# Turning two quarters of x by DMA instead of TensorE, with GpSimd normalising the last, in an attention-and-gate kernel

## The chip, the cores and the metric

The kernel runs on one core of one Trainium2 chip. The metric is the device time of one launch in microseconds, as the median of several runs. The core has five engines with an instruction stream each: TensorE (PE), VectorE (DVE), ScalarE (ACT), GpSimd (POOL) and SyncE (SP, which here only issues transfers). The engines run at the same time and wait for each other by semaphores.

## The reference

x is 2048 rows by 512 columns in bf16. It is normalised row by row, and the result goes into two branches: attention with 32 query heads of width 16 that all share one key and one value head, and a dense network with 1792 hidden columns. The output joins them.

```python
xn = _layernorm(x, axis=-1)
q = (xn @ wq)          # 32 heads of 16
k = xn @ wk            # one head of 16
v = xn @ wv            # one head of 16
scores = jnp.einsum("bhqd,bkd->bhqk", q, k) * (Dh ** -0.5)
p = _softmax(scores, axis=-1)
o = jnp.einsum("bhqk,bkd->bhqd", p, v)
s = o.transpose(0, 2, 1, 3).reshape(B, S, H * Dh) @ wo
h = _silu(xn @ w1)     # 1792 columns
g = _silu(h @ w2)
return x + s * g
```

## The kernel before

**Data.** x lies in SBUF as 16 tiles of 128 rows (`x_sb`). A quarter is four tiles, 512 rows; there are four, numbered 0 to 3 by `c` in the code. Each quarter is normalised into `xn_sb`, turned so that the columns of x lie on the partitions (`xnT_sb`), and then projected: to keys (`mm_K`, in two halves of 256 rows), to values (`mm_V`), to queries and into the dense network.

**Scores and exponentials.** Heads are worked in groups of four; four quarters of queries times eight groups give 32 groups, and each meets 16 key tiles of 128 rows. One key tile for four heads is four blocks of 128 x 512 scores, so there are 2048 blocks. TensorE computes them (L613). Two blocks side by side in one of two buffers `psA` (a "pair" below) go to ScalarE, which takes the exponential of both in one instruction (L643). Single blocks in the banks `psD` (two halves) and `psF` go to VectorE, which makes exponentials another way: it adds and clamps in int16 so that the bits form a power of two (L681), and GpSimd adds two offsets to a finished tile of four blocks (`int64_add`, L706); three weighted copies of the values make the sum close to the exponential. TensorE multiplies the exponentials by the values into `psO` (L765, a "round" is four such multiplications side by side). ScalarE also takes 72 tanh of the dense network (L1081).

**The order.** Nothing is decided at run time. A recorder, the class `Sched` and the loop behind it, goes through the whole program when the kernel is built. It keeps a model of when each engine will be free and when each result will be ready, and with it writes one fixed list of instructions and waits for each engine. In each step the loop decides what TensorE does next: another pair for ScalarE, a block for VectorE if a bank is free, a round of `psO`, a piece of the dense network, or a job of the `front` list (turn T, keys K, values V, quarter by quarter). So how many blocks ScalarE takes and how many VectorE takes falls out of the recording. The numbers that steer the decisions come from a table `RULES` of 22 rows, and a string `PLAN` names a row for each stretch of 5 us of recorded time:

```python
    STRETCH = 5
    PLAN = (
        "AAAAJAVDBHQUALNMAMMPRULHALUHROAAMAKVIAVMMASMAAAAAFVIAAKAANJM"
...
RULES[PLAN[min(int(K.act_end / STRETCH), len(PLAN) - 1)]]
```

A transfer has a `lane`, its own semaphore; in the recorder's model it takes its issuing engine 0.05 us and lands after the `cost` that is given.

**The front.** Quarter 0 is handled by hand-written calls. For the others VectorE takes statistics of each tile (L408), aggregates them (L423), GpSimd forms the reciprocal standard deviation (`rstd_pow`, L427 and L429), VectorE normalises four tiles (`normalise`, L441), TensorE turns two tiles at a time against an identity (`transposes`, L452, eight transposes into one bank), VectorE copies them out (`evac_T`, L460), TensorE projects keys (`mm_K`, L483) and VectorE copies these to `kTa_sb` (`evac_K`, L495). Four transfers on SP then move them to other partitions of `kTb_sb` (`move_K`, L501), from which every second group reads. SP also issues the weight loads (w1 at L383, wo and w2 at L386 and L387) and, after the last normalisation, reloads four x tiles for the final addition (`load_xr`, L1087).

Of the kernel before, what the change touches and what calls it, by code (L numbers as in the profile page):

```python
# [13 lines left out]
P = 128  # L14
# [21 lines left out]
class Sched:  # L36
# [107 lines left out]
    def op(self, eng, fn, reads=(), writes=(), lane=None, cost=None):  # L144
        who = lane or eng
        if lane:
            self.lanes[lane] = eng
        n = self.done.get(who, 0)
        self.done[who] = n + 1
        deps = self.deps(eng, reads, writes)  # L150
        self.at[(who, n)] = self.model(eng, lane, cost, max([self.at[d] for d in deps.items()], default=0.0))
        clk = self.clock.setdefault(eng, {})
        waits = []
        cand = [(f, m) for f, m in deps.items() if clk.get(f, -1) < m]
        for f, m in cand:
            implied = False
            for f2, m2 in cand:
                if (f2, m2) != (f, m) and self.snap[(f2, m2)].get(f, -1) >= m:
                    implied = True
            if not implied:  # L160
                waits.append((f, m))
        for f, m in cand:
            for g, k in self.snap[(f, m)].items():
                if clk.get(g, -1) < k:
                    clk[g] = k
            if clk.get(f, -1) < m:
                clk[f] = m
        for f, m in waits:
            self.flagged.setdefault(f, set()).add(m)
        self.snap[(who, n)] = dict(clk)  # L170
        self.queues.setdefault(eng, []).append((fn, waits, who, n))
        for r in reads:
            self.readers.setdefault(r, {})[who] = n
        for w in writes:
            self.last_w[w] = (who, n)
            self.readers[w] = {}
        return who, n
# [36 lines left out]
def bass_recurrent_scan__grouped_kv_mqa__dense_activation_silu__prompt_kernel(  # L214
# [16 lines left out]
    NC = S // NQ  # L231
# [20 lines left out]
    EV = "vava"  # L252
    PVWAIT, FKEEP = 0.2, 0.75
    NPAIR, LEAD_PAIR = 1, 1
    TWIN = 0
    XHOLD, XTASK, XWAIT, XGAIN, XCOST, XOPEN, XBEH, AIM = 7, 0, 0.3, 9, 1.0, 0, 99, 0.43
    TGATE, FRESH, JOINT = 0.33, 0, 0
# [20 lines left out]
        K=(0.2, 3.0, 0.65, 10, 1.2, 2.0, 0, 12, 0.2, 3, 3, 0.0, 0.15, 0.43, 0, 0.33, 0, 0),  # L278
# [14 lines left out]
    with ExitStack() as es:  # L293
# [46 lines left out]
        K = Sched()  # L340
# [63 lines left out]
        def tiles(c):  # L404
            return range(4 * c, 4 * c + 4)
# [26 lines left out]
        def rstd_sqrt(c):  # L432
# [4 lines left out]
            K.act_end += 1.28  # L437
            op("v", lambda e: e.reciprocal(rstd_sb[:, sl], rstd_sb[:, sl]), reads=[("rstd", c)], writes=[("rstd", c)], cost=0.2)

        def normalise(t, eng):  # L440
            op(eng, lambda e: e.tensor_scalar(xn_sb[:, t % 8, :], x_sb[:, t, :], mv_sb[:, t, 0:1], rstd_sb[:, t:t + 1],  # L441
                                              op0=ALU.subtract, op1=ALU.mult),
               reads=[("x", t), ("mv", t), ("rstd", t // 4)], writes=[("xn", t % 8)], cost=0.41)

        def transposes(c, half, bank, key):
            ps = bank.bitcast(BF16)
# [28 lines left out]
                op("v", lambda e: e.tensor_copy(dst, src), reads=[key], writes=[("xnT", 0, t)])  # L475

        def xnT_keys(c):
            return [("xnT", c, t) for t in range(2 if c else 4)]

        def mm_K(c, bank, key, a=0, b=NQ):  # L480
            def f(e):
# [320 lines left out]
        def ln_ag(tk):  # L802
            c = tk["c"]
            for t in tiles(c):
                aggr(t)
            rstd_pow(c)
            tok.add(("ag", c))
            if c == NC - 1:
                first_add()
                for a in shifts:  # L810
                    shift(*a)
                shifts.clear()

        def ln_nm(tk):
            t = tk["t"]
            normalise(t, "v")
            tok.add(("nm", t))
            if t == NT - 1:
                for n in range(4):
                    load_xr(n)  # L820

        for c in range(1, NC):
            if c > 1:
                for t in tiles(c):
                    task("st", ln_st, 0.687, t=t, reads=[("x", t)], writes=[])
                task("ag", ln_ag, 0.4, c=c, reads=[], writes=[], need=[("st", t) for t in tiles(c)])
            for t in tiles(c):
                task("nm", ln_nm, 0.41, t=t, reads=[("rstd", c)], writes=[], need=[("ag", c)] + ([("T", t - 8)] if t >= 8 else []))

        def on_slot(gi):  # L830
# [85 lines left out]
        jobs = [jb for _, jb in timed]  # L916
        all_slots = sum(SIZE[jb[0]] for jb in jobs)
        jobs += [("wp", tt) for tt in range(4 * (NC - 1), 4 * NC)]
        front = [("V", 0)] + [jb for c in range(1, NC) for jb in (("T", c, 0), ("T", c, 1), ("K", c, 0), ("K", c, 1), ("V", c))]
        jst = dict(open=None, part=0, bank=None, tanh=[], slots=0)  # L920

        def progress():
# [26 lines left out]
        def front_ready(jb, t):  # L949
            k, c = jb[:2]  # L950
            if k == "T":
                ts = [4 * c + 2 * jb[2] + n for n in range(2)]
                return all(("nm", n) in tok for n in ts) and K.ready("pe", [("xn", n % 8) for n in ts]) <= t + 0.2
            if k == "K":
                return ("xnT",) + jb[1:] in tok and K.ready("pe", [("xnT",) + jb[1:]]) <= t + 0.2
            return (c == 0 or all(("xnT", c, h) in tok for h in range(2))) and K.ready("pe", xnT_keys(c) + ["wv"]) <= t + 0.05

        def emit_front(jb, b):
# [561 lines left out]
```

## Time and profile before

| What | Value |
|---|---|
| Median of 2 runs | 662.22 us (662.14 to 662.3) |
| The profiled execution's own time | 662.46 us |
| Its span in the profile | 660.6 us |
| Granted TensorE clock over the span | 1.0 |
| First and last start of a ScalarE exponential (L643) | 10.2 and 652.1 us |
| Exponentials on ScalarE, and its tanh | 662 and 72 |
| Score blocks evaluated by VectorE (L681, 512 columns each) | 724 |
| VectorE normalisations (L441) of quarters 1 to 3 | 12, in steps of about 0.35 us |
| VectorE copies of turned tiles (L460) of quarters 1 to 3 | 6, 0.67 to 0.69 us each |
| First weight load (w1, 1792 KB): issue, time to landing | 15.22 us, 8.1 us |

In the rows of groups, the columns are line, engine, operation, output and inputs with shapes, and count; then busy time and mean duration of one; then the engine's idle time ahead of them and who ended it. In a table of waits they are the waiting engine and line, the engine and line waited for, the total, the number of waits and the longest. In a timeline they are start, length and the instruction with its count. In a table of stretches they are the stretch and its length, busy time and count of each engine, the granted clock, the share of the DMA engines and GB/s. The chain of work is followed back from the last instruction, at each step to what released it.

### The profile page before, as it was taken

Reading aid. Unit: us, or ns where it says so; the run is one execution under the profiler, and the core shown is the slowest. Engines: PE = TensorE matmul, PEld = TensorE weight load, DVE = VectorE, ACT = ScalarE, POOL = GpSimd, SP = SyncE. Lnnn points to the kernel's source line nnn. Section 1 sums busy time; section 2 is a strip of 40 time slices with the busy share of each in tenths; the row PEclk is TensorE's granted clock in tenths of the full one; section 3 lists DMA queues with packets and bytes.
Section 4 is the critical chain, followed back from the end, with each engine's and each line's share of the span. In section 5 each row is a group of like instructions: output and inputs, shape, how many; then the busy total and the mean of one; then the engine's idle time right before and its main releaser. Section 6 shows DMA issues by size and latency. Waiting matters only on the chain.

```text
span 660.6 us, 18424 instructions
## 1 busy us (share of the span) xinstructions
PE 648.8 (98%) x8061; PEld 182.9 (28%) x8061; DVE 597.3 (90%) x1021; ACT 652.5 (99%) x754; POOL 382.9 (58%) x387
## 2 busy tenths in 40 slices
PE   8999999999999999999999999999999999999996
PEld 4422222222222222222222222222222222222222
DVE  7998899998899989999998989999989888898996
ACT  8999999999999999999999999999999999999997
POOL 3265666655566567566656655575656555665554
PEclk9999999999999999999999999999999999999999
DMA  5440000000000000000000000010000000000110
GB/s 167 153 147 1 2 1 2 2 1 2 2 1 2 17 18 18 17 2 2 1 2 1 2 1 2 2 33 18 18 1 3 1 2 2 1 2 2 33 34 33
DMA packets 12320, 12.48 MB, mean 19 GB/s; under 512 B 2512, under 2 KB 11728, under 8 KB 12240
## 3 DMA queue, kind: packets, MB, share of 16 engines
q1 hardware_dynamic: 11680, 10.78, 5.3%
q8 instruction: 63, 1.03, 0.7%
q10 hardware_dynamic: 560, 0.52, 0.2%
q14 instruction: 17, 0.14, 0.1%
HBM read 8.95 MB, written 2.10 MB: 17 GB/s over the span
## 4 chain that ended last, share of the span: by engine, by line
ACT 91%; PE 4%; DVE 2%; issue 1%; DMA 1%; SPq 1%; POOL 0%; POOLq 0%
ACT pa_sb L643 85%; ACT t_sb L1081 5%; PE psA L613 1%; DMA x_sb<-in_A_x_dram 1%; PE psO L765 1%; DVE ph_sb L681 1%; DVE stats_sb L408 0%; POOL ph_sb L706 0%; PE psD L452 0%; PE psF L392 0%; DMA kTb_sb<-kTa_sb 0%; SPq L501 0%; PE psD L483 0%; DVE kTa_sb L495 0%; POOLq L293 0%
## 5 line engine op out<-in xcount | busy, mean ns | idle before, releaser
L643 ACT ACTIVATE pa_sb<-psA 128x1024 bf16<-128x1024 f32 x662 | 630.5, 1217 | 0.9 <-PE psA L613 0.6
L706 POOL INT64_ADD ph_sb<-ph_sb x290 | 300.3, 1048 | 192.7 <-DVE ph_sb L681 192.6
L681 DVE TENSOR_SCALAR ph_sb<-psD 128x512 int16<-128x512 f32 (+1 forms) x520 | 349.1, 689 | 33.7 <-PE psD L613 29.8
L765 PE MATMUL psO<-ph_sb,vaug_sb 128*32 128x512 bf16 x1740 | 215.9, 383 | 0.1
L765 PE MATMUL psO<-pa_sb,vaug_sb 128*32 128x512 bf16 (+1 forms) x1332 | 200.2, 383 | 0.4 <-ACT pa_sb L643 0.4
L613 PE MATMUL psA<-qT_sb,kTa_sb 32*128 32x512 bf16 x688 | 133.4, 385 | 1.9 <-DVE kTa_sb L495 0.5
L613 PE MATMUL psD<-qT_sb,kTb_sb 32*128 32x512 bf16 x353 | 129.5, 384 | 0.0
L613 PE MATMUL psA<-qT_sb,kTb_sb 32*128 32x512 bf16 x628 | 121.7, 385 | 2.2 <-ACT pa_sb L643 1.7
L613 PE MATMUL psD<-qT_sb,kTa_sb 32*128 32x512 bf16 x309 | 111.6, 384 | 0.2
L706 POOL INT64_ADD x_sb<-x_sb x72 | 74.5, 1046 | 52.2 <-DVE x_sb L681 52.1
L681 DVE TENSOR_SCALAR x_sb<-psD 128x512 int16<-128x512 f32 (+1 forms) x132 | 90.1, 690 | 10.6 <-PE psD L613 8.9
L765 PE MATMUL psO<-x_sb,vaug_sb 128*32 128x512 bf16 x432 | 73.7, 383 | 0.0
L613 PEld LDWEIGHTS psA<-qT_sb,kTa_sb 32*128 32x128 bf16 x688 | 32.3, 91 | 141.8 <-ACT pa_sb L643 125.5
L392 PE MATMUL psF<-xnT_sb,w_sb 128*32 128x512 bf16 x896 | 71.1, 385 | 0.0
L392 PE MATMUL psF<-w_sb,u_sb 128*32 128x512 bf16 x896 | 69.2, 384 | 0.0
L613 PEld LDWEIGHTS psA<-qT_sb,kTb_sb 32*128 32x128 bf16 x628 | 29.5, 91 | 134.4 <-ACT pa_sb L643 124.4
L765 PEld LDWEIGHTS psO<-ph_sb,vaug_sb 128*32 128x32 bf16 x1740 | 52.5, 95 | 49.7 <-issue 34.1
L765 PEld LDWEIGHTS psO<-pa_sb,vaug_sb 128*32 128x32 bf16 x1332 | 48.1, 94 | 41.9 <-issue 32.1
L1081 ACT ACTIVATE t_sb<-psF 128x512 bf16<-128x512 f32 x72 | 57.4, 797 | 0.0
L1113 DVE SCALAR_TENSOR_TENSOR u_sb<-t_sb,psF 128x512 bf16<-128x512 bf16 x56 | 38.0, 679 | 4.7 <-ACT t_sb L1081 4.2
L681 DVE TENSOR_SCALAR ph_sb<-psF 128x512 int16<-128x512 f32 x52 | 35.4, 681 | 0.0
L613 PEld LDWEIGHTS psD<-qT_sb,kTb_sb 32*128 32x128 bf16 x353 | 30.9, 91 | 3.5 <-DVE ph_sb L681 2.5
(128 smaller groups left out, 341.6 us busy)
## 6 DMA issues: line engine op xcount, KB each, us to landing
w_sb<-in_B_w_dram SPq DMA_DIRECT2D x2, 1792.0 KB, 8.8
x_sb<-in_A_x_dram SPq DMA_DIRECT2D x18, 128.0 KB, 2.3
out_dram<-ob_sb SPq DMA_DIRECT2D x14, 128.0 KB, 1.7
x_sb<-in_A_x_dram SPq DMA_DIRECT2D x3, 512.0 KB, 7.1
wop_sb<-in_A_wo_dram SPq DMA_DIRECT2D x1, 512.0 KB, 4.0
wq_sb<-in_A_wq_dram SPq DMA_DIRECT2D x1, 384.0 KB, 6.6
x_sb<-in_A_x_dram ACTq DMA_DIRECT2D x2, 128.0 KB, 2.9
kTb_sb<-kTa_sb SPq DMA_DIRECT2D x16, 16.0 KB, 2.3
```

The costliest lines, as they stand in the source:

```text
L392: r = e.matmul(bank[32 * i:32 * i + 32, :], lhsT=lhsT[:, 32 * i:32 * i + 32], rhs=rhs, start=start, stop=stop, tile_position=(0, 32 * i), ...
L613: return e.matmul(ap, lhsT=kT_sb[g % 2][32 * i:32 * i + 32, kt * P:(kt + 1) * P], rhs=qT_sb[32 * i:32 * i + 32, c % 2, g // 2, :], start=T ...
L643: d = op("a", lambda e: e.activation(pa_sb[:, sl, :], psA[k][:, :], ACT.Exp, scale=ESCALE), reads=["A%d" % k], writes=[("pa", sl)], cost=2 ...
L681: d = op("v", lambda e: e.tensor_scalar(ph_ap(0, sl, 512 * pos, 512 * pos + m), src, float(PH_ONE + PH_BIAS), 0.0, op0=ALU.add, op1=ALU.ma ...
L706: d = op("gp", lambda e, j=j: e.int64_add(ph_ap(j, sl, 0, 4 * NQ).bitcast(I64), ph_ap(0, sl, 0, 4 * NQ).bitcast(I64), PH_SHIFT[j] * 0x0001 ...
L765: r = e.matmul(psO[32 * i:32 * i + 32, cs], lhsT=vaug_sb[:, p["v"], p["kt"], :], rhs=p["ap"], start=s0, stop=s1, tile_position=(0, 32 * i) ...
L1081: op("a", lambda e: e.activation(t_sb[:, n % 2, :], bank_ap(b), ACT.Tanh, scale=0.5 if jb[0] == "h" else 0.25), reads=[b], writes=[("t", n ...
L1113: op("v", lambda e: e.scalar_tensor_tensor(out=dst, in0=t_sb[:, n % 2, :], scalar=1.0, in1=src, op0=ALU.add, op1=ALU.mult), reads=tk["read ...
```

## The change

Quarters 2 and 3 (the third and the fourth; `TR`) are no longer turned by TensorE. Each normalised tile of 128 x 512 is turned by one transposing transfer on SP, straight from `xn_sb` to its place in `xnT_sb`; the T jobs of these two quarters and their copies by VectorE are gone. The recorder is told that such a transfer lands after 2.6 us. The four tiles of quarter 3 (`GNORM`) are normalised by GpSimd, right behind its reciprocal deviation, instead of by VectorE, for which the recorder reckons 0.75 us each. A key projection of these quarters waits for the two turns that it reads. `PLAN` and `RULES` are not changed.

```diff
+    TR, GNORM, TRCOST = (2, 3), (3,), 2.6
...
+        def turn(t):
+
+            op("sp", lambda e: e.dma_start(xnT_sb[:, :, t * P:(t + 1) * P], xn_sb[:, t % 8, :], transpose=True),
+               reads=[("xn", t % 8)], writes=[("xnT", t // 4, t % 4)], lane=f"tr{t}", cost=TRCOST)
+
         def normalise(t, eng):
...
-               reads=[("x", t), ("mv", t), ("rstd", t // 4)], writes=[("xn", t % 8)], cost=0.41)
+               reads=[("x", t), ("mv", t), ("rstd", t // 4)], writes=[("xn", t % 8)], cost=0.41 if eng == "v" else 0.75)
...
         def xnT_keys(c):
-            return [("xnT", c, t) for t in range(2 if c else 4)]
+            return [("xnT", c, t) for t in range(2 if c and c not in TR else 4)]
+
+        def half_keys(c, h):
+            return [("xnT", c, 2 * h), ("xnT", c, 2 * h + 1)] if c in TR else [("xnT", c, h)]
...
             rstd_pow(c)
             tok.add(("ag", c))
+            if c in GNORM:
+                for t in tiles(c):
+                    normalise(t, "gp")
+                    tok.add(("nm", t))
+                    turned(t)
+                if c == NC - 1:
+                    for n in range(4):
+                        load_xr(n)
...
+        def turned(t):
+            c, h = t // 4, t % 4 // 2
+            if c in TR:
+                turn(t)
+                tok.add(("T", t))
+                if t % 2:
+                    tok.add(("xnT", c, h))
+
         def ln_nm(tk):
             t = tk["t"]
             normalise(t, "v")
             tok.add(("nm", t))
+            turned(t)
...
-            for t in tiles(c):
+            for t in tiles(c) if c not in GNORM else ():
                 task("nm", ln_nm, 0.41, t=t, reads=[("rstd", c)], writes=[], need=[("ag", c)] + ([("T", t - 8)] if t >= 8 else []))
...
-        front = [("V", 0)] + [jb for c in range(1, NC) for jb in (("T", c, 0), ("T", c, 1), ("K", c, 0), ("K", c, 1), ("V", c))]
+        front = [("V", 0)] + [jb for c in range(1, NC) for jb in ([("T", c, 0), ("T", c, 1)] if c not in TR else []) + [("K", c, 0), ("K", c, 1), ("V", c)]]
...
-                return ("xnT",) + jb[1:] in tok and K.ready("pe", [("xnT",) + jb[1:]]) <= t + 0.2
+                return ("xnT",) + jb[1:] in tok and K.ready("pe", half_keys(*jb[1:])) <= t + 0.2
```

## The prediction

> **What bounds the kernel now.** I read the page's busy times first, then the chain that ended last and who waits for whom, then one line's starts, and last the first 40 us engine by engine, since the change acts there. The page:
>
> ```profile
> span 660.6 us, 18424 instructions
> PE 648.8 (98%) x8061; PEld 182.9 (28%) x8061; DVE 597.3 (90%) x1021; ACT 652.5 (99%) x754; POOL 382.9 (58%) x387
> ACT 91%; PE 4%; DVE 2%; issue 1%; DMA 1%; SPq 1%; POOL 0%; POOLq 0%
> L643 ACT ACTIVATE pa_sb<-psA 128x1024 bf16<-128x1024 f32 x662 | 630.5, 1217 | 0.9 <-PE psA L613 0.6
> L681 DVE TENSOR_SCALAR ph_sb<-psD 128x512 int16<-128x512 f32 (+1 forms) x520 | 349.1, 689 | 33.7 <-PE psD L613 29.8
> ```
>
> PE and ACT are both nearly full by this line. The table of waits says which of them waits for the other:
>
> ```profile
> PEld psA L613 <- ACT pa_sb L643: 249.9, 585, 0.8
> ACT pa_sb L643 <- PE psA L613: 0.6, 1, 0.6
> ```
>
> PE waits 585 times for ACT to free a score buffer, 0.43 us each; ACT waits for PE once. So ACT is the bound, and the time is a count: how many exponentials ACT is given. One line's own view and two pieces of the chain give the price of one:
>
> ```profile
> L643 ACT ACTIVATE pa_sb<-psA x662: 1018/1215/1372, 10.2 to 652.1; 128x1024 bf16<-128x1024 f32 x166
> ```
>
> ```profile
> 53.29 0.49 ACT t_sb L1081
> 53.78 3.67 ACT pa_sb L643 x4
> ```
>
> The 1217 ns of the page overlap; the step is shorter. From first to last start lie 652.1 - 10.2 = 641.9 us, in which 72 tanh take 72 x 0.49 = 35.3; the other 661 steps take 606.6 / 661 = 0.918 us (3.67 / 4 says the same). In the records no step is under 0.903. The span is then 10.2 + 641.9 + 8.5 of tail. All 2048 score blocks are shared out: ACT takes two per exponential, DVE (L681) the rest. A block that DVE does not take costs ACT half a step.
>
> The front, where third and fourth quarter are turned today (columns: start, length, instruction):
>
> ```profile
> 20.16 1.38 DVE L441 TENSOR_SCALAR xn_sb<-x_sb,mv_sb,rstd_sb 128x512 bf16<-128x512 bf16 x4
> 22.06 1.44 DVE L460 COPY xnT_sb<-psD 128x1024 bf16<-128x1024 bf16 x2
> ```
>
> ```profile
> 23.04 0.39 PE L613 MATMUL psA<-qT_sb,kTa_sb 32*128 32x512 bf16 x2
> 23.36 0.61 PE L483 MATMUL psD<-xnT_sb,wkp_sb 128*128 128x256 bf16 x4
> 23.90 0.39 PE L613 MATMUL psA<-qT_sb,kTa_sb 32*128 32x512 bf16 x2
> 24.23 0.61 PE L483 MATMUL psF<-xnT_sb,wkp_sb 128*128 128x256 bf16 x4
> ```
>
> ```profile
> 15.22 0.59 SPq L383 DMA_DIRECT2D w_sb<-in_B_w_dram  x1
> 17.84 10.71 SPq L501 DMA_DIRECT2D kTb_sb<-kTa_sb  x8
> 28.60 2.00 SPq L1087 DMA_DIRECT2D x_sb<-in_A_x_dram  x4
> ```
>
> ```profile
> 20.00:22.00 2.00, 2.00 (x26) 0.85 (x22) 2.00 (x6) 2.00 (x3) 0.12 (x1) 1.00 1.00 410
> 22.00:24.00 2.00, 2.00 (x23) 1.05 (x21) 1.92 (x4) 2.00 (x3) 0.00 (x0) 1.00 0.19 61
> ```
>
> The reader is to see that PE puts each K projection between two score pairs, and that the DMA engines are full (share 1.00, 410 GB/s) with the first weight load, issued at 15.22, until about 22.4, just when the first turns will be issued.
>
> **The change, part by part.** The instruction order of both kernels can be counted on each engine.
>
> *Removed.* PE loses 32 transposes (eight take 0.55 in the chain: 2.2 us), DVE four turn copies of 0.69 and four normalisations of 0.35 (1.38 / 4): 4.2 us. Both engines stand off the path, so alone this is worth nothing; spent on six more blocks of 0.6 it would save three exponentials, 2.8 us.
>
> *The shares.* It is not spent so. The order fixes the counts: ACT goes from 662 to 679 exponentials, DVE from 724 to 690 blocks, POOL from 362 to 344 shifts. By exponential 65 DVE has taken 51 blocks in both; by 290 it is 19 behind, by 490 38, by 650 50 (the longer run then gives it 27 more blocks). The loss lies all along the run, far from the turns: the rule for each 5 us was kept, the work now stands elsewhere under those rules, and the recorder finds DVE or a bank unready more often (intervals between score pairs with no block for DVE: 54 before, 128 after). Cost: 17 x 0.918 = 15.6 us; at the floor 17 x 0.903 = 15.4. DVE's relief cannot undo it, because the order is fixed when recorded.
>
> *New long intervals.* Two intervals hold much attention-value work between score pairs: after pair 503 nine rounds of four matmuls, after pair 585 twelve; before has five at most in mid-run. In the timeline one round before the next pair takes 0.33 and two 0.55, so 0.22 a round and 0.11 beside; a score pair 0.32. That is 0.43 + 9 x 0.22 = 2.41 and 3.07 us. ACT's step is 0.92, and the spacing of 1.08 at 35.99 passed without delaying ACT, so 0.16 are covered: 1.3 + 2.0 = 3.3 us. Bounds: 2.5 (cover of 0.56, a buffer filled one wait of 0.43 earlier) and 3.6 (no cover). I take 3.2.
>
> *The turns of the third quarter.* After pair 16 the keys of two quarters are used up, and the order now has K, K and V of quarter three together ahead of pair 17; K waits for turns 8 and 9, the second K for 10 and 11, everything behind them on PE waits too. Pair 16 starts at 23.90 today and DVE's order up to the normalisation is unchanged, so the turns' sources are ready from 20.5 to 21.5. On SP they follow the four key moves that start at 17.84; an issue costs 0.51 to 0.6, so the last leaves at 22.2 to 22.8. No row shows a transposing transfer. Lower bound: 1.8 from issue to landing, the quickest key move: 24.0. Nearest row in size: 128 KB of x, 2.3 to 2.6: 24.5 to 25.4. Upper bound: the four in series after the load, 22.9 + 4 x 2.3 = 32.1. I take 25.3, the row of equal size at its late end, as the key moves issued at 17.84 took 5.6 behind that load. Then second K 25.4, plus 0.54 (K) and 0.49 (V): pair 17 at 26.4, 24.77 today: 1.6 us. At the bounds: 24.23 + 0.54 + 0.54 + 0.49 = 25.8, so 1.0 even with turns in time; and 8.4.
>
> The Trainium skill (VectorE: DVE Perf Modes, section The three transpose paths) speaks against this move: 1309 ns for 128x128 by the DMA crossbar against 390 by TensorE, which it prefers where the result may go to PSUM. By it a 128x512 turn is an estimated 5.2 us if its four blocks go in turn, and the sum would end near the second rival or above; no row here shows it.
>
> *The fourth quarter.* DVE's statistics come about 1.6 us earlier (no turn copies ahead of them), rstd at about 24.5, then POOL normalises four tiles. POOL's fills give 0.31 for 256 columns and 1.80 for 2048, so 0.52 for 512; a 256-column copy takes 0.40, so 0.8 at most by doubling. At 0.75 turn 15 leaves at 27.6 and lands by 30.2, ahead of the second K after pair 22 (about 31.2 with the shift): nothing. Without that cover it costs up to 0.7. POOL's first integer add, behind a 5.5 us wait, moves from 31.68 to about 33, no more than PE's shift: nothing.
>
> *The queue of SP.* Key moves of quarter three (25.65 today) now stand behind turn 15 and four x reloads (2.0 us): issued from about 30.2, the last landed by 35; PE asks for two of them after pair 27, 33.95 today and about 35.6 with the shift. Quarter four's leave behind them from 32.7 and land by 37; the first is asked for after pair 30, about 38.7: nothing, or 0.5 if late. Two delays of the front today, steps of 1.197 and 1.130 at exponentials 19 and 27 (0.5 together), belong to orders that are gone: -0.5.
>
> Sum: 15.6 + 3.2 + 1.6 - 0.5 = 19.9. The profiled execution took 662.46 (span 660.6 and 1.9 around it); plus 19.9 is 682.4. The median of the runs shown is 0.24 lower: 682.1, so 682.
>
> **The rivals.** *First, punctual ACT.* With fewer blocks PE and DVE have room, and the mean step falls from 0.918 towards 0.910: 679 x 0.008 = 5.4 less, 676.7. For: the floor is 0.903. Against: steps after an interval with no, one or two blocks average 0.919, 0.919 and 0.915, so fewer blocks alone do not shorten them.
>
> *Second, turns in series.* Each takes 2.3 after the one before: turn 11 at 32.1 (8.4), turn 15 at 41.3, which holds the second K of quarter four about 3 more: 8.4 + 3 in place of 1.6, 692. For: no row excludes it, and the turns' sources sit in SBUF like those of the key moves, which took 2.1 to 2.9 for an eighth of the bytes. Against: four x loads issued together landed 2.3 to 2.6 after their issue, so plain transfers do not queue so.
>
> *Third, not slower.* The one way is ACT's step: at 679 exponentials it must fall to (606.6 + 0.5) / 678 = 0.895 to equal today, and 0.903 is the shortest there is. Only if PE's transposes were what stretches each step could it come near; but in the chain after 53 us, where none run, the step is 0.918 as well. Within 2% (at most +13.2) needs 0.910 with none of the new stalls: 672.
>
> *Fourth, the change does not do what it says*: the turns are there in the order, eight on SP, so only their price is open; slower than series (5 us and more each) gives 700 and up.
>
> **How the numbers follow.** Forecast 0.70 (678.5 to 686), first rival 0.09, second 0.13, third 0.04 (most of it within 2%), fourth 0.04. The range takes in the first rival's end and most of the second: 677 to 691. A measurement of this kernel tells about 2% from no change, 649 to 675.4: faster 0.01, same 0.05, slower 0.94.
>
> **What would show it.** In the profile after: 679 exponentials with 72 tanh, mean step 0.918; one gap of 1 to 2.5 us between exponentials 16 and 17, ended by a K projection; two gaps of 1 to 2 at about 503 and 585; turns landing 2 to 3.5 us after issue; POOL's normalisation at 0.5 to 1 us. It is wrong if the mean step leaves 0.912 to 0.924, or if PE waits for turns longer than 3 us.

## The result, and the profile after

The changed kernel takes 689.22 us (median of 2 runs, 688.84 to 689.60) against 662.22: a ratio of 1.0408, with a 95% interval of 1.0363 to 1.0452. The profiled execution took 689.6, its span is 687.4. That lies in the range of 677 to 691, but above the likeliest case's own range of 678.5 to 686. Lines are numbered anew: the exponential is L652, the score product L622, the turn L443, the normalisation L447, the key projection L492.

The page after; ahead of the chain of work stands the granted clock in 40 slices of 17.2 us:

```profile
span 687.4 us, 18461 instructions
PE 666.0 (97%) x8096; PEld 186.0 (27%) x8101; DVE 579.7 (84%) x958; ACT 669.1 (97%) x771; POOL 371.9 (54%) x373
PEclk9779999999999999999999999999999999999999
ACT 87%; PE 9%; DVE 2%; DMA 1%; SPq 0%; issue 0%
L652 ACT ACTIVATE pa_sb<-psA 128x1024 bf16<-128x1024 f32 x679 | 646.4, 1211 | 11.3 <-PE psD L622 8.6
L690 DVE TENSOR_SCALAR ph_sb<-psD 128x512 int16<-128x512 f32 (+1 forms) x492 | 340.4, 709 | 65.2 <-PE psD L622 52.7
```

There are 679 exponentials, as counted from the order, and VectorE's share of the work fell. New are 11.3 us in which ACT stood idle ahead of an exponential (0.9 before), the rise of PE in the chain from 4% to 9%, and a clock that is not full in the second and third slice. The table of waits says the same of ACT, and names one wait that did not exist:

```profile
PEld psA L622 <- ACT pa_sb L652: 263.0, 610, 0.8
ACT pa_sb L652 <- PE psD L622: 8.6, 7, 3.8
ACT pa_sb L652 <- PE psA L622: 2.1, 4, 0.6
PE psD L492 <- DMA xnT_sb<-xn_sb: 2.4, 2, 1.5
```

ACT is still the bound over the run (610 waits of PE for it), but now it was ACT that waited, eleven times by these two lines. Where, the timeline of ACT shows for the front:

```profile
14.83 10.28 ACT L652 ACTIVATE pa_sb<-psA 128x1024 bf16<-128x1024 f32 x11
28.89 1.02 ACT L652 ACTIVATE pa_sb<-psA 128x1024 bf16<-128x1024 f32 x1 [3.78 <-PE psD L622]
30.40 1.02 ACT L652 ACTIVATE pa_sb<-psA 128x1024 bf16<-128x1024 f32 x1 [0.49 <-PE psA L622]
31.91 1.02 ACT L652 ACTIVATE pa_sb<-psA 128x1024 bf16<-128x1024 f32 x1 [0.49 <-PE psD L622]
...
42.06 6.69 ACT L652 ACTIVATE pa_sb<-psA 128x1024 bf16<-128x1024 f32 x7 [0.50 <-PE psD L622]
```

One gap of 3.78, and behind it, up to 42.06, a row of gaps of 0.5. In before the same stretch is one row of 37 exponentials with no gap:

```profile
14.23 34.47 ACT L643 ACTIVATE pa_sb<-psA 128x1024 bf16<-128x1024 f32 x37
```

The timeline of PE in after, and the table of stretches of 2 us (busy time by engine, granted clock, DMA share, GB/s), say what made both:

```profile
23.46 0.39 PE L622 MATMUL psA<-qT_sb,kTa_sb 32*128 32x512 bf16 x2
24.74 0.60 PE L492 MATMUL psD<-xnT_sb,wkp_sb 128*128 128x256 bf16 x4 [0.89 <-DMA xnT_sb<-xn_sb]
26.88 1.01 PE L492 MATMUL psD<-xnT_sb,wkp_sb 128*128 128x256 bf16 x4 [1.55 <-DMA xnT_sb<-xn_sb]
...
30.29 1.04 PE L393 MATMUL psO<-zero_sb 128*32 128x512 bf16 x8
```

```profile
24.00:26.00 2.00, 0.60 (x4) 0.32 (x4) 0.42 (x1) 1.11 (x2) 1.89 (x2) 1.00 0.57 116
26.00:28.00 2.00, 1.12 (x15) 0.90 (x15) 0.07 (x1) 0.00 (x0) 2.00 (x2) 0.57 0.29 59
28.00:30.00 2.00, 2.00 (x25) 0.56 (x21) 1.46 (x3) 1.02 (x1) 2.00 (x2) 0.50 0.33 67
...
40.00:42.00 2.00, 2.00 (x19) 0.29 (x15) 1.29 (x2) 1.07 (x2) 0.84 (x1) 0.50 0.10 25
42.00:44.00 2.00, 2.00 (x22) 0.48 (x19) 1.51 (x3) 1.88 (x2) 1.12 (x2) 0.67 0.64 169
```

PE waits for turns 0.89 and 1.55 us. The same four matmuls of a key projection take 0.60 before the second wait and 1.01 after it: the granted clock goes to 0.50 at 26.26, and it stays there until 43.33 (0.67 over the last stretch), although PE is busy all the time from 28 on. The eight zero products between two score pairs take 0.97 in the chain instead of 0.55, a pair 0.54 instead of 0.32; the interval is 1.51 instead of 0.86, so it passes ACT's 0.903 and ACT waits.

The cause of the two waits is on SP (its timeline, then two lines of the view of the turned tile):

```profile
20.29 13.47 SPq L443 DMA_TRANSPOSE xnT_sb<-xn_sb  x8
```

```profile
L443 SPq DMA_TRANSPOSE xnT_sb<-xn_sb x8: 1189/1258/1325, 20.3 to 32.6; - x8
DMA to landing us min/median/max: 2.4/2.5/4.1
```

In the median a turn lands 2.5 us after its issue begins, as forecast, but SP needs 1.26 us to issue one, where plain transfers of the same queue take 0.5 to 0.6. So the four of the third quarter leave at 20.3, 21.7, 23.0 and 24.3, and the last lands at 26.75.

GpSimd's timeline, and two places late on ACT's:

```profile
24.26 8.28 POOL L447 TENSOR_SCALAR xn_sb<-x_sb,mv_sb,rstd_sb 128x512 bf16<-128x512 bf16 x4
...
38.04 0.18 POOL L588 INT64_ADD scr_i<-scr_i  x1 [5.50 <-issue]
```

```profile
510.44 1.94 ACT L652 ACTIVATE pa_sb<-psA 128x1024 bf16<-128x1024 f32 x2 [1.03 <-PE psD L622]
...
591.96 1.02 ACT L652 ACTIVATE pa_sb<-psA 128x1024 bf16<-128x1024 f32 x1 [1.84 <-PE psD L622]
```

A normalisation on GpSimd takes 8.28 / 4 = 2.07 us, not 0.75. The last two lines are the two long intervals that the order showed, at exponentials 503 and 585.

**Where the time went.** One sum carries the rest. From the starts of all exponentials of a profiled execution, with 0.477 us taken out for each tanh between two of them, come steps of 0.903 at least. The time from the first exponential to the last is then 0.903 for each step, the tanh, and what the steps have above 0.903, which can be added up by stretches of the run:

| profiled execution | exponentials | above floor, to the 17th | the next 25 steps | the rest | first to last |
|---|---|---|---|---|---|
| before | 662 | 0.64 | 0.56 | 9.44 | 641.87 |
| after | 679 | 4.25 | 5.26 | 12.68 | 668.77 |

The difference of 26.9 is 17 x 0.903 = 15.35 for the count, 3.6 up to the gap (the gap alone is 3.97), 4.7 behind it, 3.24 in the rest. The span grew by 26.8.

### The profile page after: what moved, and what is told of

The parts are those of the page before. It is cut to its first block, busy times and chain, and to the rows that moved or that the text cites. A ratio compares the mean times of both kernels' runs of the same rounds, so it can differ in the third digit from the quotient of the medians.

```text
span 687.4 us, 18461 instructions
## 1 busy us (share of the span) xinstructions
PE 666.0 (97%) x8096; PEld 186.0 (27%) x8101; DVE 579.7 (84%) x958; ACT 669.1 (97%) x771; POOL 371.9 (54%) x373
## 4 chain that ended last, share of the span: by engine, by line
ACT 87%; PE 9%; DVE 2%; DMA 1%; SPq 0%; issue 0%
ACT pa_sb L652 82%; ACT t_sb L1107 5%; PE psA L622 3%; PE psO L774 3%; PE psF L393 1%; DVE stats_sb L409 1%; DMA x_sb<-in_A_x_dram 1%; PE psO L393 1%; PE psD L492 1%; DMA xnT_sb<-xn_sb 0%; SPq L443 0%; PE psA L668 0%; DVE xn_sb L447 0%; DVE kTa_sb L504 0%; PE psD L458 0%
## 5 line engine op out<-in xcount | busy, mean ns | idle before, releaser
L652 ACT ACTIVATE pa_sb<-psA 128x1024 bf16<-128x1024 f32 x679 | 646.4, 1211 | 11.3 <-PE psD L622 8.6
L715 POOL INT64_ADD ph_sb<-ph_sb x276 | 285.0, 1045 | 234.6 <-DVE ph_sb L690 234.5
L690 DVE TENSOR_SCALAR ph_sb<-psD 128x512 int16<-128x512 f32 (+1 forms) x492 | 340.4, 709 | 65.2 <-PE psD L622 52.7
L774 PE MATMUL psO<-ph_sb,vaug_sb 128*32 128x512 bf16 x1656 | 203.2, 383 | 0.1
L774 PE MATMUL psO<-pa_sb,vaug_sb 128*32 128x512 bf16 (+1 forms) x1366 | 195.7, 387 | 0.6 <-DVE onb_sb L903 0.6
L622 PE MATMUL psA<-qT_sb,kTa_sb 32*128 32x512 bf16 x696 | 137.3, 391 | 5.5 <-ACT pa_sb L652 3.6
L622 PE MATMUL psA<-qT_sb,kTb_sb 32*128 32x512 bf16 x654 | 126.8, 385 | 6.0 <-ACT pa_sb L652 5.3
L622 PE MATMUL psD<-qT_sb,kTb_sb 32*128 32x512 bf16 x335 | 116.0, 387 | 0.3
L622 PE MATMUL psD<-qT_sb,kTa_sb 32*128 32x512 bf16 x313 | 103.2, 386 | 0.2
L715 POOL INT64_ADD x_sb<-x_sb x68 | 70.3, 1046 | 48.9 <-DVE x_sb L690 48.9
L622 PEld LDWEIGHTS psA<-qT_sb,kTa_sb 32*128 32x128 bf16 x696 | 32.7, 91 | 149.4 <-ACT pa_sb L652 132.8
L622 PEld LDWEIGHTS psA<-qT_sb,kTb_sb 32*128 32x128 bf16 x654 | 30.7, 91 | 140.6 <-ACT pa_sb L652 130.2
L774 PEld LDWEIGHTS psO<-ph_sb,vaug_sb 128*32 128x32 bf16 x1656 | 51.0, 95 | 47.6 <-issue 32.7
L622 PEld LDWEIGHTS psD<-qT_sb,kTb_sb 32*128 32x128 bf16 x335 | 27.6, 91 | 4.0 <-DVE ph_sb L690 3.1
L622 PEld LDWEIGHTS psD<-qT_sb,kTa_sb 32*128 32x128 bf16 x313 | 24.7, 91 | 3.1 <-DVE ph_sb L690 2.5
```

Of the source, the lines that this page charges most:

```text
L622: return e.matmul(ap, lhsT=kT_sb[g % 2][32 * i:32 * i + 32, kt * P:(kt + 1) * P], rhs=qT_sb[32 * i:32 * i + 32, c % 2, g // 2, :], start=T ...
L652: d = op("a", lambda e: e.activation(pa_sb[:, sl, :], psA[k][:, :], ACT.Exp, scale=ESCALE), reads=["A%d" % k], writes=[("pa", sl)], cost=2 ...
L690: d = op("v", lambda e: e.tensor_scalar(ph_ap(0, sl, 512 * pos, 512 * pos + m), src, float(PH_ONE + PH_BIAS), 0.0, op0=ALU.add, op1=ALU.ma ...
L715: d = op("gp", lambda e, j=j: e.int64_add(ph_ap(j, sl, 0, 4 * NQ).bitcast(I64), ph_ap(0, sl, 0, 4 * NQ).bitcast(I64), PH_SHIFT[j] * 0x0001 ...
L774: r = e.matmul(psO[32 * i:32 * i + 32, cs], lhsT=vaug_sb[:, p["v"], p["kt"], :], rhs=p["ap"], start=s0, stop=s1, tile_position=(0, 32 * i) ...
```

## The experiments

The theory after the result: the time is lost in two independent ways. The order was planned for other numbers and gives ACT 16 or 17 exponentials more whatever the turns do; and the turns, issued at 1.26 us each, leave PE idle long enough that its clock is halved, which stretches what follows. The rivals stand with each run. The same sums for all runs, from their profiled executions (the named times are medians, with the ratio to before on the same chip):

| run | exponentials | to the 17th | next 25 | rest | median us | ratio, 95% interval |
|---|---|---|---|---|---|---|
| e1_nudge | 678 | 0.68 | 0.56 | 11.21 | 678.96 | 1.0256, 1.0240 to 1.0271 |
| e7_before_flat | 680 | 0.20 | 0.77 | 9.60 | 678.69 | 1.0252, 1.0234 to 1.0270 |
| e8_after_flat | 679 | 4.31 | 5.89 | 9.65 | 685.03 | 1.0351, 1.0326 to 1.0376 |
| e12_search | 675 | 4.66 | 2.90 | 10.06 | 681.22 | 1.0272, 1.0255 to 1.0289 |
| e2_busy | 679 | 5.24 | 3.06 | 12.71 | 688.54 | 1.0408, 1.0385 to 1.0431 |
| e3_w1_late | 679 | 4.11 | 7.07 | 12.71 | 691.92 | 1.0452, 1.0435 to 1.0469 |
| e4_turn_only | 681 | 4.05 | 6.94 | 12.30 | 693.00 | 1.0468, 1.0445 to 1.0492 |
| e5_gap | 662 | 4.10 | 2.57 | 9.43 | 670.59 | 1.0119, 1.0095 to 1.0142 |
| e6_gap_busy | 662 | 5.01 | 0.44 | 9.43 | 666.87 | 1.0073, 1.0057 to 1.0089 |
| e9_same_order | 662 | 3.71 | 6.62 | 9.46 | 672.74 | 1.0150, 1.0135 to 1.0165 |
| e10_same_order_busy | 662 | 3.13 | 7.97 | 9.39 | 673.05 | 1.0182, 1.0130 to 1.0233 |
| e11_same_order_gp | 662 | 0.98 | 10.11 | 9.45 | 672.08 | 1.0142, 1.0127 to 1.0157 |

### Is the count a matter of the turns? e1_nudge, e7_before_flat, e8_after_flat, e12_search

e1 is the kernel before with one number of the recorder's model changed, and no instruction added or taken away on purpose:

```diff
-               reads=[("x", t), ("mv", t), ("rstd", t // 4)], writes=[("xn", t % 8)], cost=0.41)
+               reads=[("x", t), ("mv", t), ("rstd", t // 4)], writes=[("xn", t % 8)], cost=0.40)
```

> The kernel before, with one number of the recorder's model changed (a normalisation by VectorE reckoned at 0.40 us and not 0.41) and no work added, removed or moved to another engine by hand; the recording then gives ScalarE 678 exponentials and not 662. Theory (the rules by stretches only fit the recording they were chosen for, so any shift costs the exponentials): 662.2 + 16 x 0.919 = 676.9, range 675.5 to 679, clock 1.0 throughout. Rival (the exponentials rise in the changed kernel because of what it does to the engines): 662 here, since nothing is done to them.

Measured: 678.96. Its page has 16 exponentials more than before, no idle time to speak of, and a full clock in every slice:

```profile
span 677.4 us, 18398 instructions
PEclk9999999999999999999999999999999999999999
L643 ACT ACTIVATE pa_sb<-psA 128x1024 bf16<-128x1024 f32 x678 | 643.9, 1195 | 1.8 <-PE psD L613 0.9
```

16 x 0.903 = 14.45 and 1.8 above the floor give the 16.25 between first and last. A hundredth of a microsecond in one reckoned duration costs 2.5%: the rules chosen for each 5 us fit the one recording that they were chosen for, and this one small change loses what they gave. So the count rises without a turned quarter; whether turned quarters add to it, the next two runs say.

e7 and e8 take that plan away from both kernels: every 5 us get the first rule.

```diff
-    PLAN = (
-        "AAAAJAVDBHQUALNMAMMPRULHALUHROAAMAKVIAVMMASMAAAAAFVIAAKAANJM"
...
+    PLAN = "A"
```

> The kernel before, with the first rule in every stretch in place of the chosen string; no work changed. The recording gives ScalarE 680 exponentials. Theory (what the chosen string is worth is 18 exponentials): 662.1 + 18 x 0.919 = 678.7, range 677 to 681. Rival (the string also keeps the steps short, so the mean step rises): above 682.

> The changed kernel with the first rule in every stretch. The recording gives ScalarE 679 exponentials, against 680 for the kernel before under the same rule. Theory (under equal rules the change itself costs the stall for the turns and the slow clock behind it, 9.4 us in the changed kernel, and saves next to nothing): 9 to 10 over the kernel before with the same rule, so 687 to 689. Rival (the changed front costs exponentials by itself): equal counts speak against it already; a time over 690 would bring it back through longer steps.

Measured: 678.69 and 685.03, with 680 and 679 exponentials. Under equal rules the turned quarters add none, so the rival, that the count comes from them, falls. Without a plan the change costs 6.3 (medians). In the profiled executions it is 8.9: the gap and the half clock behind it take 9.2 more, the one exponential fewer 0.9 less, and the rest of the two runs is alike (9.60 and 9.65, the long intervals are gone). The 6.3 is below the 9 to 10 that were expected; these were reckoned from one execution of after, and here too the profiled execution, at 687.4, was the longest of the four and had the longest half clock (mean clock 0.987, the others 0.989 to 0.995).

e12 is the changed kernel with another `PLAN`, searched for its own numbers by changing letters and keeping the recordings with fewer exponentials:

```diff
-    PLAN = (
-        "AAAAJAVDBHQUALNMAMMPRULHALUHROAAMAKVIAVMMASMAAAAAFVIAAKAANJM"
...
+    PLAN = "AAIAAAVDJHQUNLCMAMMJRUIHALUHROAAMAKVIAVMMASMAAAAAFVIAAKAANIMAIGHQLHSNAMAAIMPOCVAQAMAAVIRAHLAMRIIAFHKAOLENETNLUAAAAPAIHRAESJAAABAATAAAAAA"
```

> The changed kernel with the string of rules searched anew for it for some eight minutes of recordings (one stretch after the other, the best of 22 rules each); no other change. The recording gives ScalarE 675 exponentials in place of 679. Theory (the count carries the shares, the front keeps its stall and slow clock): 662.1 + 13 x 0.919 + 9 to 10, so 682 to 685, without the two long intervals of the changed kernel. Rival (the string fits the order and not the chip): no better than the one rule throughout, 685 to 689.

Measured: 681.22, a little below the 682 to 685 expected, 8 less than after and 19 more than before: 675 exponentials, no long interval, but still gaps of 1.2 and 2.8 above the floor and four steps of 1.5. A short search gets back 4 of the 17. Whether a long one finds 662 is open.

### What set the gap? e3_w1_late, e2_busy, e4_turn_only

The prediction saw the turns behind the 1.8 MB weight load on the DMA engines. e3 issues this load behind the third quarter's turns:

```diff
         move_K(0)
         load_w1()
+        w1_late = K.queues["sp"].pop()
...
             turned(t)
+            if t == 11:
+                K.queues["sp"].append(w1_late)
```

> The changed kernel with the load of w1 issued behind the four turns of the third quarter and not ahead of them; all else as recorded. Theory (the turns are late because SP takes 1.3 us to issue each, one after the other): the first turn lands 2.5 us after its issue and not 4.0, the fourth still at about 26.8, the gap on ACT at exponential 16 stays at 4 to 5 us, time 689 within 1. Rival, as the prediction had it (they queue on the DMA engines behind the load): the fourth lands 1.5 to 2 us earlier, and the gap and the slow clock shrink: 683 to 687.

Measured: 691.92, where 689 within 1 was expected. Without the load the first turn lands 2.5 us after its issue instead of 4.0, yet turn 11 lands at 26.67 instead of 26.75, and the gap is 3.97 above the floor in both. So SP's issuing sets the gap, not the load: the rival that the prediction held falls. The load itself now stands in the way of the fourth quarter's turns (view of the turned tile), which is the 1.8 more in the next 25 steps:

```profile
L443 SPq DMA_TRANSPOSE xnT_sb<-xn_sb x8: 1257/1361/1969, 20.2 to 32.5; - x8
...
DMA to landing us min/median/max: 2.5/3.2/8.5
```

e2 keeps PE busy in its waits with zero products, 4, 7 and 8 of them, ahead of three key projections, so that the clock should stay. The recorder does not reckon them, so the order is that of after:

```diff
+    BUSY = {(2, 0): 4, (2, 1): 7, (3, 1): 8}
...
             elif k == "K":
+                if (c, jb[2]) in BUSY:
...
+                    warm(BUSY[c, jb[2]], ap, b)
...
                 mm_K(c, ap, b, jb[2] * 256, jb[2] * 256 + 256)
```

> The changed kernel in its own order, with products of zeros put on PE ahead of three key projections that wait for turns: 4 and 7 ahead of the two of the third quarter, 8 ahead of the second of the fourth; they write the bank that the projection then overwrites. Theory (PE idle for about 3 us around 23.9 to 26.9 us halves the granted clock, and the nine steps of 1.5 us that follow are that clock): clock 1.0 throughout, no series of 1.5 us steps, the stall at exponential 16 still about 4 us; 9 x 0.6 = 5.5 less, of which up to 1.8 comes back as a wait for the last turn, which lands at about 35.0: 684 to 686. Rival (the 1.5 us steps come from turns and key moves disturbing the memory while they run): steps stay at 1.5, 689.

Measured: 688.54, not the 684 to 686 expected, and near the 689 of the rival. The half clock shrank to 3.4 us (three long steps of 1.29 to 1.51 instead of eight of 1.5), but turn 11 landed 3.9 us after its issue this time, at 28.42, so that PE idled 1.5 us all the same, the clock fell at 30.07, and the gap grew by 0.8; and the 8 products stood ahead of a projection whose turns had already landed: a step of 2.5. The shorter row of long steps is for the theory; the time settles nothing, and what delayed turn 11 is open. Turn 12 of after landed as late, 4.1.

e4 leaves the normalisation with VectorE: `GNORM = ()`.

> The changed kernel without the part for GpSimd: the fourth quarter is normalised by VectorE again, both quarters are still turned by transfers. The recording gives ScalarE 681 exponentials, 2 more than the changed kernel. Theory (shares by the recording, the stall of the third quarter and the slow clock behind it; GpSimd's slow normalisation is hidden in the changed kernel by that slow clock): stall at exponential 16 as before, 689.2 + 2 x 0.919 less the two long intervals of the changed kernel where this order lacks them: 687 to 692. Rival (GpSimd's 2.07 us a tile is what holds the front back): 683 to 686.

Measured: 693.00, one more than the 687 to 692 expected, with 681 exponentials. The gap is there (3.4 above the floor) and so is the half clock, so GpSimd's part did not make them; the rival falls. The rest of the extra time is two exponentials more, and turns 14 and 15, which in this order stand behind key moves on SP (one step of 3.6).

### Does an idle PE halve the clock? e5_gap, e6_gap_busy

Both have the order, the counts and the TensorE turns of before. In e5 the second key projection of the third quarter waits for three plain copies in series, begun when tile 11 is normalised: a PE wait as in after, with no transposing transfer anywhere.

```diff
             normalise(t, "v")
+            if t == 11:
+                op("sp", lambda e: e.dma_start(fin_sb[:, 0, :], xn_sb[:, 3, :]), reads=[("xn", 3)], writes=[("fin", 0)], lane="gap0")
+                op("sp", lambda e: e.dma_start(fin_sb[:, 1, :], fin_sb[:, 0, :]), reads=[("fin", 0)], writes=[("fin", 1)], lane="gap1")
+                op("sp", lambda e: e.dma_start(fin_sb[:, 0, :], fin_sb[:, 1, :]), reads=[("fin", 1)], writes=[("fin", 0)], lane="gap2")
...
+            if c == 2 and b == NQ:
+                rd = rd + [("fin", 0)]
```

e6 adds 18 zero products ahead of that projection.

> The kernel before in its own order, with no turn by transfer at all: three plain copies of 128 KB within SBUF, each behind the one before, start from tile 11's normalised rows at about 21.6 us, and the second key projection of the third quarter also waits for the last of them, at about 28.5; so PE is idle for some 4 us from about 24.2. Theory (an idle PE halves the granted clock, and it stays halved for some 16 us whatever made PE idle): a stall of about 4 us and then 8 to 10 steps of ScalarE at 1.5 us in place of 0.92, 5 to 6 us more: 671 to 673. Rival (the slow steps belong to the transposing transfers): the stall alone, 666 to 667.

> As the kernel with three copies behind each other, but PE does 18 products of zeros (about 3.9 us) ahead of the projection that waits, so it is busy through nearly all of the wait. Theory (idle PE sets the clock): the stall of about 4 us stays, no step of 1.5 us follows, clock 1.0: 666 to 667. Rival (the late projection and the work piled up behind it make the slow steps): 671 to 673 as without the products.

Measured: 670.59 for e5, just below the 671 to 673 expected, and 666.87 for e6, as expected. The projection behind the wait, from the timelines of PE, and the stretch after it, first e5:

```profile
27.16 0.97 PE L483 MATMUL psF<-xnT_sb,wkp_sb 128*128 128x256 bf16 x4 [3.35 <-DMA fin_sb<-fin_sb]
```

```profile
28.00:30.00 2.00, 2.00 (x14) 0.35 (x13) 1.67 (x4) 1.02 (x1) 0.00 (x0) 0.50 0.06 15
...
36.00:38.00 2.00, 2.00 (x38) 0.87 (x35) 1.98 (x4) 2.00 (x3) 0.84 (x1) 1.00 0.03 8
```

then e6:

```profile
23.87 4.06 PE L399 MATMUL psF<-zero_sb 128*128 128x512 bf16 x18
28.78 0.61 PE L483 MATMUL psF<-xnT_sb,wkp_sb 128*128 128x256 bf16 x4 [0.85 <-DMA fin_sb<-fin_sb]
```

```profile
28.00:30.00 2.00, 1.22 (x15) 0.53 (x15) 0.57 (x2) 0.25 (x1) 0.00 (x0) 1.00 0.18 61
```

With PE idle for 3.35 us the projection behind takes 0.97 and the clock is 0.50; with the products in the wait it takes 0.61 and the clock is full, though ACT's gap is 0.9 longer. No step behind the gap is long in e6. So the idle PE halves the clock, not the turns, their writes or their place. e6 is 3.7 us shorter than e5 in the medians, for 0.9 of longer gap in the profiled executions: by these an estimated 4.6 us was the price of the half clock. In e5's profiled execution the half clock lasts 6.8 us, and the 25 steps behind the gap take 2.1 more than e6's. The other three runs of e5, whose traces are not kept, are 3 us longer (670.6 against 667.76), and their mean clocks of 0.986 to 0.989 mean, by (1 - mean clock) x 669 / 0.5, an estimated 15 to 19 us of it.

### The front alone, in the old order: e9, e10, e11

These three keep before's order of every instruction on PE, ACT, VectorE and GpSimd (662 exponentials). In e9 both quarters are also turned by transfers, from which the key projections read; TensorE's transposes and VectorE's copies stay, into a buffer that nobody reads, and VectorE normalises.

```diff
             normalise(t, "v")
+            if t // 4 in TR:
+                op("sp", lambda e: e.dma_start(xnT_sb[:, :, t * P:(t + 1) * P], xn_sb[:, t % 8, :], transpose=True),
+                   reads=[("xn", t % 8)], writes=[("xnD", t)], lane=f"tr{t}")
...
+            rd = rd + [("xnD", 4 * c + a // P + n) for n in range((b - a) // P) if c in TR]
             op("pe", f, reads=rd + ["wkp"], writes=[key], cost=("full", [None] * NDC, b - a))
```

e10 is e9 with 5, 8, 9 and 7 zero products ahead of the four key projections. e11 is before with one change only: GpSimd normalises the fourth quarter.

> Both quarters are turned by transfers and the key projections wait for them, but the instructions of PE, ACT, DVE and GpSimd are in exactly the order of the kernel before (662 exponentials): PE's transposes and DVE's copies of these quarters are still done, into a buffer nobody reads, so their work is not saved; VectorE normalises. Theory (of the 27 us some 17 are the recording and some 9 the turns with the slow clock behind them): turns issued 1.3 us apart hold the projections of the third quarter by about 3 us and of the fourth by up to 4, part of it hidden by the slow clock: 670 to 675. Rival (the turns disturb the whole run): 680 and more.

> As the kernel with turns in the order of before, with 5, 8, 9 and 7 products of zeros on PE ahead of the four waiting projections. Theory (PE kept busy keeps the clock): no steps of 1.5 us or three at most, the waits of the third and fourth quarter remain: 667 to 671, 2 to 5 less than without the products. Rival (the clock costs little where the waits follow each other anyway): same as without, within 1.

> The order of the kernel before on PE, ACT and SP; only the four normalisations of the fourth quarter go to GpSimd, behind its reciprocal deviation; PE turns all quarters as before. GpSimd took 2.07 us a tile in the changed kernel, so tiles 13 and 15 are ready at about 30.3 and 34.4, where PE asks for them at 27.0 and 28.2. Theory (GpSimd's part is not free, it was hidden behind the late turns and the slow clock): a stall of about 3 and one of about 4 us, and slow steps behind them: 671 to 676. Rival (as the prediction had it, covered): 662 to 663.

e9: 672.74, 10.1 more than before, as expected: that is what turns and clock cost with the count left alone, and with e1's 16.8 for the count it makes the 27 of the whole change. The two were measured apart, and 10.1 + 16.8 = 26.9; how near that is owes something to chance, since neither order is after's.

e10: 673.05 (three runs of 672.5 to 673.2 and one of 680.3), no gain, where 667 to 671 was expected. The clock stayed full until 44.41, but there are still 8.0 us above the floor in the 25 steps, as other waits: for turns of the fourth quarter, steps of 3.9 and 2.6 behind exponentials 21 and 22, and for key moves, 2.5 behind 27, with 3.4 us of half clock after that one. Exponential 23 starts 1.1 us earlier than in e9 (37.95 against 39.07), exponential 31 later (48.19 against 47.73): what the full clock gained was lost again at the next wait. Its rival (where waits follow one another the clock is worth little) is the better reading here, against e6, where one wait stood alone.

e11: 672.08. GpSimd's part alone costs 9.4 us, as expected from its 2.07 us a tile. Its timeline on GpSimd, and its table of waits:

```profile
26.52 8.27 POOL L441 TENSOR_SCALAR xn_sb<-x_sb,mv_sb,rstd_sb 128x512 bf16<-128x512 bf16 x4
```

```profile
PE psF L452 <- POOL xn_sb L441: 3.6, 1, 3.6
...
PE psD L452 <- POOL xn_sb L441: 2.5, 1, 2.5
```

PE waits 3.6 and 2.5 us for the tiles, the steps are 5.05 and 4.05, and the clock goes to 0.50 here too, from about 31.4 to 45, with no transposing transfer in the kernel. In after this price is hidden: the half clock had put the second key projection of the fourth quarter at 36.34, and turn 15 had landed at 34.97.

No run here is faster than before.

## Why the prediction was right or wrong

**The count, +15.6: right.** 17 exponentials, 15.35 at the floor; e1 and e7 show the same loss in kernels without a single transposing transfer. The reasoning (the order is fixed when recorded, so VectorE's relief is not spent) holds. The first rival, a punctual ACT, falls: behind the front and without the two long intervals the steps are 12.68 - 3.5 = 9.2 above the floor, 9.4 before. So does the third, not slower: no step is below 0.903. Still, one of the prediction's own signs of being wrong came up: taken as it took the mean step, this is (668.77 - 35.3) / 678 = 0.934, outside 0.912 to 0.924 (its own sum gives 0.924). The excess stands in the front; behind it and without the two long intervals the mean is 0.917.

**The long intervals, +3.2: right.** The steps are 2.30 and 3.03, so 1.40 + 2.12 = 3.5 above the floor, against 3.3 worked out; e8, which has none, is 3.0 lower in the rest of the run.

**The turns of the third quarter, +1.6: the mis-sized term.** The step that failed is "an issue costs 0.51 to 0.6, so the last leaves at 22.2 to 22.8": the key moves' row was taken for a transposing transfer, and there it was 1.26. The last left at 24.3. The other half, 2.5 from issue to landing, was right, and so was the place. The gap came out at 3.97, where the prediction looked for 1 to 2.5: beyond its 1.6 stand 1.5 for the later landing, 0.33 and 0.22 for projections and a pair at half clock; the remaining 0.3 is that exponential 16, from which the gap is counted, starts at 24.02 and not at 24.39 as in before. The Trainium skill (VectorE: DVE Perf Modes, section The three transpose paths) gave 1309 ns for 128x128 on the DMA path, an estimated 5.2 for a tile in series; the trace does not agree as to the landing, 2.5 for all four blocks, and the measurement decides. For the second rival this means no: the third quarter's landings lie 1.3 apart at most, by SP's issuing, not 2.3.

**The clock: missing altogether.** No term, no rival and no bound of the prediction had it, and it is 4.7 of the 26.9, net of the two old delays (5.26 above the floor in the 25 steps behind the gap, where before had 0.56). The rows that it shows held no halved clock: before's is 1.00 there. What it could have seen is the margin: eight zero products and a pair take 0.86 at full clock, so PE in the front has 0.04 to spare against 0.903, and nothing that slows PE is covered there. The prediction asked only what PE waits for, not at what speed it goes on. Before's own trace had a hint: over 650 to 661 us, where PE runs out of work, the granted clock is 0.96.

**The fourth quarter, 0: wrong in size, right in effect, by luck.** GpSimd takes 2.07 us a tile, above the bound of 0.8 that rows of fills and of a copy gave; this normalisation, with two operands for each partition, was not like either. Turn 15 was issued at 32.6, not 27.6. At full clock, with pairs 0.92 apart from 28.24, the second key projection would have come at about 33.2 and waited some 1.8 us for it (an estimate from these rows); e11 shows what it costs without cover: waits of 3.6 and 2.5 us. The named cover, the projection's late place, was there only because of the half clock.

**SP's queue, 0, and the two old delays, -0.5: as predicted in cost.** The steps of 1.197 and 1.130 are gone. The key moves of both quarters left from 35.85, not 30.2 and 32.7, behind turn 15 and the four reloads, and PE still waited for none of them; in e10, with its full clock up to there, it waited 1.6 for one, so the half clock covered here as well, as far as these runs tell. The first integer add came at 38.04, not 33, and no exponential waited for it.

So 15.6 + 3.2 were right to 0.3, and the front was put at 1.1 where it cost 8.3. That the range held is luck: it is owed to its upper end, which was drawn for the second rival, by a mechanism that did not occur.

## What to carry to other kernels

A static order that was tuned piece by piece is part of the kernel's numbers: an edit that shifts its model can throw the tuning away (here 0.01 us did: 16 exponentials, 2.5%), so count the bound engine's instructions in the new order before anything else, and plan anew. A transfer has two prices, the queue's for issuing and the way to landing; several on one queue follow one another at the first. Where PE is close to the bound, a wait can cost more than itself, as those of 1.5 to 3.6 us did here: look at the granted clock in the stretches behind it, and at what runs at half speed there.

## What was not expected of the hardware

- Issuing a transposing transfer of 128x512 holds SP for 1.26 us (1.19 to 1.33 in after), against 0.5 to 0.6 for a plain one; it lands 2.5 us after the issue began, at times 3.9 to 4.1.
- PE idle for long enough halves the granted clock, and it can come back late. Here it was 0.50 for a whole number of times 3.41 us: once in e2 and e10, twice in e5, three times in e12, four times in e11, five times (17.1) in after, e3, e8 and e9, once and three times in e4. In the 3.41 us ahead of each of these falls PE had been idle, by the records, for 1.54 (e2) to 3.31 us (e5), in one piece or more; in after, 1.81. Of the other stretches of this length at full clock, counted from the same changes in all 14 traces, none with more than 1.20 us of idle PE stayed without a fall, but for one of 1.79 near the end of after. The Trainium skill (TensorE: Matmul & The Clock Gate, section Part 1: The HAM clock gate) lets the clock go down after an idle window of about 3.4 us and come back after about 3.4 us of sustained work. The first agrees with e5, but elsewhere about half as much idle time was enough; the second agrees with e2 and e10, but not with 7 us in e5 and 15 in after of busy PE at 0.50. What ends the half clock is open, and no run tried the idle time step by step.
- GpSimd's normalisation of 128x512 bf16 with two operands for each partition takes 2.07 us, six times VectorE's 0.35.
- In e10 the half clock and the waits behind it did not add up: with the clock kept full over the first of them, waits of the same size came out.
